# Batch 0 in two halves by queries: sparse attention and an ELU layer pair on one Trainium2 core

## The chip, the core and the metric

The kernel runs on one core of one Trainium2 chip. The metric is device microseconds (us) from the launch's first to its last work, and less is better. A run of the profiler gives one execution's trace; times of other executions are taken without it. Names of engines as in the profile: PE is the matmul engine (PEld its weight loads), DVE the vector engine, ACT the scalar engine, POOL and SP the two that issue most of the transfers. "DMA" is the set of 16 transfer engines.

## What is computed

Eight batches of 576 tokens with 8 heads of 64 go through attention with two fixed masks; the result, 4608 tokens of 512, goes through two dense layers with an ELU between them.

```python
mask_local = (rel >= 0) & (rel < 32)                       # heads 0..3
mask_strided = (rel >= 0) & (pos[None, :] % 32 == pos[:, None] % 32)   # heads 4..7
attn = softmax(where(mask, q @ k.T / 8, -1e9));  x = attn @ v
h = x @ w_in                                               # 4608x512 @ 512x2048
out = where(h > 0, h, exp(min(h, 0)) - 1) @ w_out          # 2048x512
```

Inputs and output are float32; the kernel computes in bf16 and loads with a cast on the way.

## The kernel before

**Tiling.** A token is numbered p*8+s with s in 0..7 (`NS`) and p in 0..71 (`RS`). Strided heads attend only within groups of equal token number modulo 32, local heads within a band of 32. A batch has four head pairs: `s0`, `s1` (strided) and `l0`, `l1` (local); each pair's queries are taken in two parts u = 0, 1. For batches 0 and 1 (`NPE`), q and k are transposed on PE (L409) and copied out of PSUM by ACT or DVE (L427); for batches 2 to 7 SP issues transposing transfers (`dma_T`, L670). Scores go to PSUM (`scores` L444, `scores_packed` L469), ACT takes the exponential (L498, L518), DVE multiplies by the mask (L504, L524), PE multiplies by v and by ones (`pv` L590), ACT takes log and exp(-log) of the sums (L622, L628), and DVE writes the scaled product into `xT` (`write_x` L634), the left operand of layer 1.

Layer 1 (`l1`, L682) works in nine chunks of 512 tokens. A chunk has 16 row blocks m of `w_in`; each takes 4 matmuls of 512 columns into one of the eight PSUM banks. ACT takes exp (L692), ACT or DVE clamps (L697), DVE takes the maximum with h (L707) and writes `g`, of which there are two tiles. Layer 2 (`l2`, L717) takes 16 matmuls of 512 columns for 128 tokens, needs all four quarters of `w_out`, and ends in a copy by ACT or DVE (L725) into one of four output buffers (`p_osb`) and a store (L731), which SP issues as two or three transfers, since the rows of a token group lie apart in the output.

**Order.** Nothing is scheduled by a planner at run time. `ORDER` (L37 to L145) is a list of about 2,600 tokens; each engine runs its instructions in the order in which the tokens stand there, and semaphores do the rest. The letters:

- D load (POOL issues it), X transposing transfer (SP), K/k cast of q/k by DVE/ACT, T transposes on PE, c/C copies of them by DVE/ACT
- S or P scores, e exp, m mask, O product with v, n log, r exp(-log), x write of x, V and W copies of v, F fills of masks and ones
- L (a and b its halves) layer 1, h exp, i/j clamp on DVE/ACT, g the maximum; Z layer 2 by quarters of the sum, o/q its copy by ACT/DVE, t its store; Y and y the last 128 tokens by halves of the output's columns
- w.7.28: 28 matmuls of zeros into bank 7

So `L.1.8.1` is chunk 1, m = 8, bank 1, and `Z.0.2.3.7` is tokens 256 to 383 of chunk 0, last quarter, bank 7. The token order couples things that do not depend on each other: a load that waits holds POOL's next loads, and a store that waits for its copy holds SP's next transposing transfers.

**Loads.** q and k of batch 0's first two strided heads come in float32 through SP and ACT in four transfers (L304), and are cast on the chip. All else is issued by POOL, in the order batch 0, most of batch 1, `w_in` (L266), `w_out`, batch 2 and so on. POOL has eight completion semaphores in rotation, so a load waits until the one eight before it has landed. SP's stores and transposing transfers have eight of their own.

In `before` batch 0 is loaded by pairs of heads, with all 72 rows p (80 where memory allows). Layer 1 of chunk 0 needs the first 512 tokens of batch 0 in the order s-major, so all four head pairs with both u.

Of the kernel before, what the change touches and what calls it, by code (L numbers as in the profile page):

```python
# [8 lines left out]
F32 = mybir.dt.float32  # L9
BF16 = mybir.dt.bfloat16  # L10
# [5 lines left out]
S = 576  # L16
D = 64
HG = 4
# [11 lines left out]

NPE = 2
# [11 lines left out]
T.1s1.q.7 r.0s1.0 x.0s1.0 e.0s0.1 c.1s1.q D.vl1.0 m.0s0.1 T.0l0.q.2 c.0l0.q O.0s0.0.34 D.vl0.0
r.0s1.1 x.0s1.1 n.0s0.0 O.0s0.1.67 n.0s0.1 r.0s0.0 S.0l0.1.01 x.0s0.0 F.k1 S.0l1.0.23 e.0l0.1
T.1s0.k.0 r.0s0.1 V.0.0 S.0l0.0.45 V.0.1 m.0l0.1 e.0l1.0 m.0l1.0 C.1s0.k O.0l1.1.23 e.0l0.0 D.kl.1
x.0s0.1 T.1l0.k.0 n.0l1.1 r.0l1.1 m.0l0.0 O.0l1.0.67 O.0l0.0.45 D.ql.1 D.wi0.0 c.1l0.k n.0l1.0
O.0l0.1.01 D.wj0.0 x.0l1.1 r.0l1.0 n.0l0.0 r.0l0.0 D.wi2.0 n.0l0.1 T.1l1.q.2 x.0l1.0 c.1l1.q r.0l0.1
D.vs.1 x.0l0.0 T.1l0.q.3 S.1s0.0.67 a.0.0.2 c.1l0.q x.0l0.1 e.1s0.0 T.1s1.k.5 a.0.1.3 b.0.0 m.1s0.0
T.1l1.k.4 C.1s1.k S.1s1.0.01 c.1l1.k S.1s0.1.67 b.0.1 h.0.0 a.0.3.4 b.0.3 e.1s0.1 a.0.2.7 i.0.0
h.0.1 g.0.0 D.wi1.0 S.1l0.0.56 e.1s1.0 h.0.3 S.1s1.1.01 m.1s0.1 i.0.1 m.1s1.0 e.1s1.1 e.1l0.0  # L50
D.wi3.0 b.0.2 h.0.2 g.0.1 a.0.9.2 b.0.9 D.vl.1 a.0.11.3 i.0.3 b.0.11 m.1s1.1 g.0.3 D.wo0.0 h.0.9
j.0.9 O.1s0.1.01 O.1s0.0.45 n.1s0.0 i.0.2 g.0.2 a.0.8.6 b.0.8 D.wo1.0 a.0.10.7 b.0.10 h.0.11 m.1l0.0
r.1s0.0 n.1s0.1 D.wo2.0 g.0.9 a.0.5.2 i.0.11 b.0.5 x.1s0.0 g.0.11 h.0.8 a.0.6.3 b.0.6 D.wo3.0
S.1l1.0.45 r.1s0.1 x.1s0.1 a.0.7.0 b.0.7 a.0.13.1 b.0.13 h.0.10 i.0.8 i.0.10 h.0.5 j.0.5 g.0.8 h.0.6
g.0.5 j.0.6 e.1l1.0 h.0.13 a.0.4.2 g.0.10 D.qs.2 g.0.6 m.1l1.0 V.1 i.0.13 b.0.4 S.1l0.1.34 h.0.7
S.1l1.1.56 e.1l0.1 e.1l1.1 i.0.7 a.0.12.7 b.0.12 D.ql.2 a.0.14.3 b.0.14 a.0.15.6 g.0.13 h.0.12
O.1s1.1.45 g.0.7 h.0.4 m.1l1.1 i.0.4 g.0.4 h.0.14 Z.0.0.0.0 b.0.15 n.1s1.1 r.1s1.1 x.1s1.1 j.0.12
g.0.12 h.0.15 O.1l0.0.12 D.ks.2 i.0.15 O.1s1.0.45 m.1l0.1 i.0.14 n.1l0.0 r.1l0.0 x.1l0.0 g.0.14
n.1s1.0 r.1s1.0 Z.0.0.1.0 X.qs.2 x.1s1.0 Z.0.2.0.7 Z.0.2.1.7 Z.0.2.2.7 g.0.15 D.kl.2 O.1l1.1.56
n.1l1.1 X.ks.2 O.1l1.0.34 n.1l1.0 r.1l1.1 x.1l1.1 X.ql.2 O.1l0.1.12 Z.0.0.2.0 Z.0.0.3.0 Z.0.2.3.7  # L60
n.1l0.1 X.kl.2 r.1l0.1 x.1l0.1 r.1l1.0 D.vs.2 x.1l1.0 L.1.8.1 L.1.5.2 h.1.5 L.1.14.3 i.1.5 h.1.8
L.1.15.4 o.0.2 h.1.14 g.1.5 L.1.7.5 q.0.0 L.1.4.2 j.1.14 i.1.8 g.1.14 L.1.10.0 h.1.4 L.1.2.3 h.1.2
h.1.7 L.1.3.7 i.1.4 D.qs.3 g.1.8 L.1.6.1 L.1.0.6 g.1.4 L.1.13.2 i.1.7 i.1.2 g.1.7 F.mx h.1.3 h.1.10
D.ks.3 g.1.2 j.1.10 D.vl.2 Z.0.3.0.5 Z.0.3.1.5 h.1.15 j.1.15 g.1.15 h.1.0 j.1.3 g.1.3 Z.0.1.0.4
X.qs.3 g.1.10 L.1.11.3 L.1.1.0 i.1.0 h.1.6 i.1.6 h.1.13 Z.0.1.1.4 Z.0.1.2.4 g.1.0 j.1.13 g.1.6
D.kl.3 h.1.11 g.1.13 h.1.1 i.1.1 g.1.1 t.0.2 j.1.11 P.2.4.67 e.2p.4 m.2p.4 P.2.1.12 e.2p.1 Z.0.1.3.4
o.0.1 Z.0.3.2.5 P.2.2.67 e.2p.2 P.2.3.01 g.1.11 W.2 P.2.0.34 m.2p.1 m.2p.2 e.2p.0 Z.0.3.3.5 m.2p.0
e.2p.3 m.2p.3 L.1.12.6 h.1.12 L.1.9.7 O.2s0.0.23 O.2s0.1.01 q.0.3 h.1.9 i.1.9 j.1.12 g.1.9 Z.1.0.0.4
Z.1.0.1.4 Z.1.3.0.5 n.2s0.0 g.1.12 t.0.0 r.2s0.0 x.2s0.0 n.2s0.1 O.2s1.0.67 r.2s0.1 n.2s1.0 r.2s1.0
V.2 Z.1.3.1.5 O.2l0.1.23 x.2s0.1 x.2s1.0 n.2l0.1 r.2l0.1 Z.1.0.2.4 Z.1.0.3.4 O.2s1.1.67 Z.1.3.2.5  # L70
t.0.3 n.2s1.1 r.2s1.1 O.2l1.1.01 q.1.0 x.2l0.1 Z.1.1.0.4 n.2l1.1 r.2l1.1 O.2l1.0.23 n.2l1.0 r.2l1.0
Z.1.1.1.4 x.2s1.1 O.2l0.0.67 Z.1.1.2.4 Z.1.1.3.4 D.ql.3 n.2l0.0 r.2l0.0 x.2l1.1 X.ks.3 P.3.4.01
e.3p.4 Z.1.3.3.5 x.2l1.0 x.2l0.0 L.2.11.0 h.2.11 q.1.1 m.3p.4 i.2.11 g.2.11 L.2.15.4 t.0.1 L.2.6.2
h.2.15 i.2.15 g.2.15 X.kl.3 X.ql.3 h.2.6 L.2.2.3 P.3.1.01 h.2.2 q.1.3 P.3.3.67 i.2.2 L.2.10.4
L.2.5.5 e.3p.1 D.vs.3 D.vl.3 j.2.6 L.2.4.0 h.2.10 m.3p.1 L.2.7.1 D.qs.4 g.2.2 D.kl.4 W.3 e.3p.3
h.2.4 j.2.4 g.2.6 O.3s0.1.67 n.3s0.1 r.3s0.1 i.2.10 g.2.10 L.2.1.2 h.2.1 g.2.4 L.2.13.3 L.2.9.0
h.2.7 m.3p.3 j.2.7 t.1.1 x.3s0.1 Z.1.2.0.4 P.3.2.67 D.ks.4 Z.1.2.1.4 i.2.1 g.2.1 g.2.7 L.2.8.1
D.ql.4 h.2.5 j.2.5 h.2.13 L.2.3.2 t.1.3 e.3p.2 g.2.5 h.2.8 i.2.13 g.2.13 h.2.3 P.3.0.56 e.3p.0
X.qs.4 L.2.0.3 h.2.0 i.2.8 g.2.8 j.2.0 h.2.9 X.ks.4 X.ql.4 m.3p.2 Z.1.2.2.4 Z.1.2.3.4 O.3l1.0.56
X.kl.4 n.3l1.0 i.2.3 g.2.3 O.3l0.1.12 D.vs.4 n.3l0.1 L.2.14.7 g.2.0 i.2.9 g.2.9 r.3l0.1 q.1.2  # L80
Z.2.0.0.3 r.3l1.0 Z.2.1.0.0 D.vl.4 m.3p.0 h.2.14 j.2.14 x.3l0.1 L.2.12.4 h.2.12 O.3s1.1.12 Z.2.0.1.3
x.3l1.0 n.3s1.1 g.2.14 r.3s1.1 O.3l1.1.67 i.2.12 Z.2.1.1.0 g.2.12 D.ks.5 n.3l1.1 r.3l1.1 O.3s1.0.45
n.3s1.0 t.1.0 Z.2.0.2.3 x.3s1.1 x.3l1.1 r.3s1.0 Z.2.0.3.3 O.3s0.0.12 n.3s0.0 x.3s1.0 P.4.4.67
Z.2.1.2.0 O.3l0.0.45 q.2.0 D.ql.5 Z.2.1.3.0 r.3s0.0 e.4p.4 P.4.2.67 n.3l0.0 x.3s0.0 r.3l0.0 m.4p.4
# [733 lines left out]
```

## Time and profile before

| | us |
|---|---|
| median of 3 runs (307.39 to 309.43) | 308.45 |
| the profiled execution, its own time | 308.96 |
| its span, first to last instruction | 307.3 |
| PE busy | 296.8 |
| ACT busy | 231.8 |
| DVE busy | 222.5 |
| POOL busy | 81.2 |
| first layer 1 matmul starts at | 23.26 |
| last matmul ends at | 303.2 |

The profile has a page (busy time, the span in 40 slices of 7.7 us, the chain of work that ended last, groups of instructions by line), and views that are asked of the trace: the timeline (merged instructions in order of time), busy time by stretches, waits. PE's busy time counts the modelled length of each matmul, 380 ns for 512 columns, while consecutive ones start much closer together; what PE has to spare is read from the distances between starts, not from the busy share.

### The profile page before, as it was taken

How to read it: one execution, taken by the hardware profiler on the slowest of the kernel's cores; microseconds unless marked ns; L12 is line 12 of the kernel's file. 1: busy time of each engine (PE TensorE's matmuls, PEld its weight loads, DVE VectorE, ACT ScalarE, POOL GpSimd, SP SyncE). 2: the span in 40 equal slices, each digit the busy share in tenths (PEclk: the TensorE clock that was granted, in tenths of full speed). 3: DMA queues.
4: the chain of work that ended last, by engine and by line, in shares of the span. 5: the costliest groups of instructions: out<-in, count | busy, mean ns of one | idle time of the engine just before them, and what ended most of it. 6: DMA issues, size and time to landing. Idle time of an engine off the chain costs nothing.

```text
span 307.3 us, 6136 instructions
## 1 busy us (share of the span) xinstructions
PE 296.8 (97%) x2316; PEld 151.8 (49%) x2316; DVE 222.5 (72%) x418; ACT 231.8 (75%) x396; POOL 81.2 (26%) x111
## 2 busy tenths in 40 slices
PE   5999999999999979999999999999999999999994
PEld 5774444445544545445444554544545544444452
DVE  4688993888689986998796777788678458973220
ACT  3798975779979997988897999966897459655321
POOL 8764323484083046092030092000000000000000
PEclk9999999999999999999999999999999999999999
DMA  8999999999999999999999199560020012101124
GB/s 156 198 195 206 195 202 160 213 198 167 234 119 139 125 162 152 228 126 128 185 151 155 36 131 152 65 156 14 20 73 0 20 51 68 36 0 34 36 68 137
DMA packets 107655, 37.58 MB, mean 122 GB/s; under 512 B 89099, under 2 KB 103147, under 8 KB 107627
## 3 DMA queue, kind: packets, MB, share of 16 engines
q0 software_dynamic: 70192, 19.43, 65.3%
q1 hardware_dynamic: 36998, 17.37, 30.0%
q10 hardware_dynamic: 436, 0.40, 0.5%
q8 instruction: 18, 0.29, 0.4%
q14 instruction: 11, 0.08, 0.1%
HBM read 39.47 MB, written 9.44 MB: 159 GB/s over the span
## 4 chain that ended last, share of the span: by engine, by line
PE 77%; DMA 9%; DVE 5%; ACT 2%; issue 2%; SPq 2%; POOL 2%; ACTq 0%; POOLq 0%; DVEq 0%
PE ps L687 34%; PE ps L721 33%; DMA kTl<-kl 4%; DMA ql<-in_q_dram 4%; PE ps L493 2%; PE ps L577 2%; SPq L680 2%; DVE xT L657 2%; DMA g<-in_q_dram 1%; PE ps L584 1%; PE ps L747 1%; PE ps L466 1%; POOL kl L243 1%; ACT ln L626 1%; PE ps L423 1%
## 5 line engine op out<-in xcount | busy, mean ns | idle before, releaser
L687 PE MATMUL ps<-xT,w_in_sb 128*128 128x512 bf16 x576 | 134.2, 380 | 0.4 <-DVE g L715 0.2
L721 PE MATMUL ps<-w_out_sb,g 128*128 128x512 bf16 x560 | 131.9, 379 | 0.0
L695 ACT ACTIVATE he<-ps 128x512 f32<-128x512 f32 x144 | 81.9, 595 | 24.2 <-PE ps L687 23.1
L687 PEld LDWEIGHTS <-w_in_sb 128*128 128x128 bf16 x576 | 54.2, 98 | 62.4 <-issue 1.1
L721 PEld LDWEIGHTS <-g 128*128 128x128 bf16 x560 | 52.4, 98 | 58.0
L715 DVE TENSOR_TENSOR g<-he,ps 128x512 bf16<-128x512 bf16 x95 | 64.0, 682 | 2.1
L657 DVE TENSOR_TENSOR xT<-ps,ln 64x576 bf16<-64x576 f32 (+1 forms) x64 | 43.3, 678 | 21.0 <-ACT ln L632 20.0
L704 DVE TENSOR_SCALAR he<-he 128x512 bf16<-128x512 f32 x95 | 40.4, 434 | 18.2 <-ACT he L695 17.7
L626 ACT ACTIVATE ln<-ps 64x576 f32<-64x576 f32 (+1 forms) x64 | 37.1, 584 | 11.7 <-PE ps L577 5.1
L632 ACT ACTIVATE ln<-ln 64x576 f32<-64x576 f32 (+1 forms) x64 | 39.7, 622 | 1.7
L713 DVE SCALAR_TENSOR_TENSOR g<-he,ps 128x512 bf16<-128x512 bf16 x49 | 32.9, 682 | 8.3 <-ACT he L702 8.0
L702 ACT ACTIVATE he<-he 128x512 bf16<-128x512 f32 x49 | 30.5, 629 | 2.6 <-DVE g L715 1.2
L502 ACT ACTIVATE e<-ps 128x1008 bf16<-128x1008 f32 (+1 forms) x30 | 27.0, 934 | 5.2 <-PE ps L493 5.1
L236 POOL DMA_DIRECT2D ql<-in_q_dram x24 | 20.1, 845 | 17.7 <-DMA qTl<-ql 11.9
L243 POOL DMA_DIRECT2D kl<-in_k_dram x24 | 17.9, 752 | 17.8 <-DMA kTl<-kl 13.4
L727 ACT COPY osb<-ps 128x512 f32<-128x512 f32 x17 | 9.9, 585 | 14.8 <-PE ps L721 14.7
L515 DVE TENSOR_TENSOR pm<-e,mask_x 128x1008 bf16<-128x1008 bf16 x24 | 16.2, 677 | 6.8 <-ACT e L502 6.8
L727 DVE COPY osb<-ps 128x512 f32<-128x512 f32 x18 | 12.3, 686 | 8.9 <-PE ps L721 8.8
L522 ACT ACTIVATE e<-ps 72x576 bf16<-72x576 f32 (+1 forms) x16 | 10.0, 646 | 2.4 <-PE ps L466 2.1
L577 PEld LDWEIGHTS <-vsp 72*128 72x128 bf16 x192 | 9.1, 98 | 5.2 <-issue 0.4
L584 PEld LDWEIGHTS <-vl 128*128 128x128 bf16 x144 | 8.6, 97 | 5.6 <-issue 0.6
L230 POOL DMA_DIRECT2D vs<-in_v_dram x8 | 5.4, 680 | 22.3 <-DVE vsp L667 21.0
(94 smaller groups left out, 177.6 us busy)
## 6 DMA issues: line engine op xcount, KB each, us to landing
out_dram<-osb SPq DMA_DIRECT2D x31, 144.0 KB
w_out_sb<-in_moe_w_out_dram POOLq DMA_DIRECT2D x4, 512.0 KB, 17.8
vl<-in_v_dram POOLq DMA_DIRECT2D x7, 288.0 KB, 11.2
ql<-in_q_dram POOLq DMA_DIRECT2D x24, 72.0 KB, 6.6
kl<-in_k_dram POOLq DMA_DIRECT2D x24, 72.0 KB, 5.4
qs<-in_q_dram POOLq DMA_DIRECT2D x5, 320.0 KB, 8.5
ks<-in_k_dram POOLq DMA_DIRECT2D x5, 320.0 KB, 7.2
vs<-in_v_dram POOLq DMA_DIRECT2D x5, 320.0 KB, 8.3
```

The lines of the kernel that those rows point to most:

```text
L502: nc.scalar.activation(e[0:R, :, 0:n], tiles.pop(("S", key, j))[0:R], ACT.Exp, scale=scale)
L626: nc.scalar.activation(t, s_ps, ACT.Ln)
L632: nc.scalar.activation(t, t, ACT.Exp, scale=-1.0)
L657: nc.vector.tensor_mul(dst, o_ps, rc)
L687: nc.tensor.matmul(tiles["h", ch, m], lhsT=w_in_sb[:, c, m * 128:(m + 1) * 128], rhs=xT[:, c, ch * CHUNK:(ch + 1) * CHUNK], start=(c == 2) ...
L695: nc.scalar.activation(e, tiles["h", i[0], i[1]], ACT.Exp)
L702: nc.scalar.activation(e1, e, ACT.Relu, bias=1.0, scale=-1.0)
L704: eng.tensor_scalar(e1, e, scalar1=1.0, scalar2=1.0, op0=ALU.min, op1=ALU.subtract)
L713: nc.vector.scalar_tensor_tensor(dst, e1, -1.0, h, op0=ALU.mult, op1=ALU.max)
L715: nc.vector.tensor_tensor(dst, e1, h, op=ALU.max)
L721: nc.tensor.matmul(ops, lhsT=g[ch % 2][:, m, kk * 128:(kk + 1) * 128], rhs=w_out_sb[:, m, :], start=(m == 0), stop=(m == MC - 1), skip_gro ...
L727: eng(o_sb, tiles.pop(("o", int(ch), int(kk))))
```

## The change

Batch 0 is cut by queries into p < 32 (`RA`, 256 tokens) and 32 <= p < 72 (`RB`, 320 tokens). Since a query sees only earlier tokens, the first half needs only the first 32 rows of q, k and v. Each half is loaded, transposed, scored and written to `xT` by itself, in the column order half, s, p. The first half packs the four heads on the partitions (4 x 32 rows), for which there are new masks. Layer 1 runs in chunks of 256, 320, 448 and then seven of 512; layer 2 stays at 128 tokens. `g` becomes one ring of 1024 columns.

The raw halves of batch 0 lie in `w_out_sb`, so the loads of `w_out` follow their transposes; batch 1's raw strided v lies in the raw buffer of local k, which batch 2 uses next. The first 256 columns of `w_in` are loaded first of all on POOL; then come half 0, `w_in` and half 1 in turns, `w_out`, and batch 1 among and behind it. The 28 matmuls of zeros go. The list of tokens is new from end to end.

```diff
+RA = PRE
+RB = RS - RA
+NA = NS * RA
+NB = NS * RB
+CH = ((0, NA), (NA, NB), (S, 2 * CHUNK - S)) + tuple(
+    (i * CHUNK, CHUNK) for i in range(2, 9))
...
-K.q.1 D.qs1.0 F.ms w.7.28 k.q.0 k.k.0 T.0s0.q.0.0 T.0s0.q.1.1 T.0s1.q.5 c.0s0.q.0 k.k.1 T.0s0.k.2.1
...
+D.wi0.0 k.k T.0s.k.6.0 K.q F.ms T.0s.q.2.0 C.0s.k.0 c.0s.q.0 S.0s.0.67 e.0s.0 F.sa D.kl0.0
+T.0l.k.2.0 D.ql0.0 D.vl0.0 D.vs0.0 m.0s.0 D.vl1.0 D.ks1.0 F.m1 F.ml T.0l.q.0.0 c.0l.q.0 D.wj0.0 F.la
+F.lb C.0l.k.0 S.0l1.0.01 e.0l1.0 V.0.0 F.k1 m.0l1.0 S.0l0.0.67 e.0l0.0 O.0s.0.34 m.0l0.0 n.0s.0
+r.0s.0 x.0s.0 O.0l.0.67 T.0s.k.5.1 c.0s.k.1 n.0l.0 D.qs1.0 D.wi1.0 r.0l.0 T.0s.q.0.1 C.0s.q.1 x.0l.0
+L.0.1.2 V.0.1 L.0.2.3 L.0.3.4 h.0.1 S.0s0.1.01 i.0.1 g.0.1 S.0s1.1.56 h.0.2 i.0.2 g.0.2 h.0.3 i.0.3
...
-Z.8.0.3.6 Z.8.2.2.1 Z.8.2.3.1 Y.8.3.0.7 q.8.2 o.8.0 y.8.3.0 t.8.2 Z.8.1.1.4 Z.8.1.2.4 t.8.0
-Z.8.1.3.4 o.8.1 t.8.1 Y.8.3.1.5 y.8.3.1
...
+t.7.1 i.9.6 g.9.6 Z.8.1.1.0 Z.8.2.1.1 Z.8.0.1.3 Y.8.3.0.2 o.7.2 Z.8.0.2.3 Z.8.0.3.3 Z.8.2.2.1
+Z.8.2.3.1 o.8.0 t.7.2 y.8.3.0 t.8.0 o.8.2 Z.8.1.2.0 Z.8.1.3.0 o.8.1 Y.8.3.1.4 q.7.3 t.7.3 t.8.2
+y.8.3.1 t.8.1
...
-    g = [consts.tile([128, MC, CHUNK], BF16, tag=f"g{i}", name=f"g{i}") for i in range(2)]
+    g = consts.tile([128, MC, 2 * CHUNK], BF16, tag="g", name="g")
...
-    raw1["vs"] = g[1][0:RP, 0:HG * NS * D // CHUNK, :].rearrange("p a b -> p (a b)")
-    stage = g[0][0:RP, 0:8, :].rearrange("p a b -> p (a b)").bitcast(F32)
+    raw1["vs"] = raw["kl"][0:RP]
+
+    part = ({nm: w_out_sb[:, i, :] for i, nm in enumerate(("qs", "ks", "ql", "kl", "vs"))},
+            {nm: w_out_sb[0:2 * RB, 8 + 2 * i:10 + 2 * i, :]
+             for i, nm in enumerate(("qs", "ks", "ql", "kl"))})
+    stage = {nm: g[:, i, :].bitcast(F32) for i, nm in enumerate("qk")}
...
+    def load_first(nm, u):
+        x = {"q": q, "k": k, "v": v}[nm[0]]
+        if nm == "vl":
+            n = HG * LB // 2
+            nc.gpsimd.dma_start(
+                out=blocks(vl_t[0], HG * LB)[PRE:128, u * n:(u + 1) * n],
+                in_=v[0, 2 * u:2 * u + 2].rearrange("h (t p) d -> p (h t) d", p=LQ))
+        elif nm == "vs":
+            if u == 0:
+                nc.gpsimd.dma_start(out=part[0][nm], in_=rows_first(x, nm))
+            else:
+                load_runs(nm, 0)
+        elif u == 0:
+            for i in range(2):
+                nc.gpsimd.dma_start(out=part[0][nm][2 * RA * i:2 * RA * (i + 1)],
+                                    in_=pair_first(x, nm, i, 0, RA))
+        else:
+            for i in range(2):
+                nc.gpsimd.dma_start(out=part[1][nm][:, i], in_=pair_first(x, nm, i, RA, RB))
...
-    for u in range(2):
-        load_stage(nc.sync, 0, u, q)
-        load_stage(nc.scalar, 1, u, k)
+    nc.sync.dma_start(out=stage["q"], in_=rows_first(q, "qs"))
+    nc.scalar.dma_start(out=stage["k"], in_=rows_first(k, "ks"))
...
+    def scores_first(key, u, bk):
+        i, j = int(bk[0]), int(bk[1])
+        p0, R = half(u)
+        c = key[1]
+        n = NA // 2 if key == "0s" else NS * R
+        sc = tiles["S", key, u] = ps[:, i:j + 1:j - i, 0:n]
+        qt, kt = qT[0][c], kT[0][c]
+        if key == "0s":
+            for sp in range(NS // 2):
+                for h in range(HG):
+                    for z in range(2):
+                        pr = slice(z * D, (z + 1) * D)
+                        q0 = (h * NS // 2 + sp) * RS
+                        k0 = h // 2 * KSY + (h % 2 * NS // 2 + sp) * RS
+                        nc.tensor.matmul(
+                            sc[h * RA:(h + 1) * RA, z, sp * RA:(sp + 1) * RA],
+                            lhsT=kt[pr, k0:k0 + RA], rhs=qt[pr, q0:q0 + RA],
+                            start=True, stop=True, skip_group_check=True)
+            return
...
     def l1(ch, m, cs, bk=None):
         ch, m = int(ch), int(m)
+        c0, n = CH[ch]
         if bk is not None:
-            tiles["h", ch, m] = ps[:, int(bk), :]
+            tiles["h", ch, m] = ps[:, int(bk), 0:n]
         for c in cs:
             nc.tensor.matmul(
                 tiles["h", ch, m], lhsT=w_in_sb[:, c, m * 128:(m + 1) * 128],
-                rhs=xT[:, c, ch * CHUNK:(ch + 1) * CHUNK],
+                rhs=xT[:, c, c0:c0 + n],
                 start=(c == 2), stop=(c == 1), skip_group_check=True)
```

The functions for transposes, copies, exponentials, masks, products and writes of batch 0 have such a second form each (`transposes_first`, `copy_first`, `exp_first`, `mask_first`, `pv_first`, `write_first`), which works on one half. In counts of PE instructions: batch 0 has 88 transposes for 96, 92 score matmuls for 56 and 108 products for 72; layer 1 has 640 matmuls (64 each of 256, 320 and 448 columns, 448 of 512) for 576; the 28 of zeros are gone; layer 2 and batches 1 to 7 keep theirs.

Elsewhere in the new list: the transposing transfers of a batch stand behind other stores than before. Before, `X.kl.3` follows the store `t.0.1`, whose copy comes after nearly all of layer 1 of chunk 1; after, it follows `t.0.0`, and `t.1.3` is the last store before batch 4's four transposing transfers. At the end, the copy `q.7.3` stands behind `Y.8.3.1` and takes the output buffer that the store `t.8.0` reads; on SP, `t.7.3`, `t.8.2`, the last half's store and `t.8.1` follow it, nine transfers in all.

More of the change, by code (lines that the diff above doesn't have):

```diff
@@ L43 @@
[L43 to L48, printed above, removed]
@@ L278, in load @@
         elif b == 0:
-            y = int(what[2])
-            if nm == "vl":
-                load_vpair(0, y)
-            else:
-                load_runs(nm, 0, 2 * y, 2)
+            load_first(nm, int(what[2]))
         elif nm == "vl":
@@ new lines, in pv_local_first @@
+    def pv_local_first(y, u, o, s):
+        p0, R = half(u)
+        pm = tiles.pop(("pm", f"0l{y}", u))
+        vb = blocks(vl_t[0], HG * LB)
+        for x in range(2):
+            nc.tensor.matmul(s[x * D:(x + 1) * D], lhsT=ones, rhs=pm[:, x],
+                             start=True, stop=True, skip_group_check=True)
+        for w, p, m in items_first(u):
+            for x in range(2):
+                ov, pv_ = (z.rearrange("k (s p) -> k s p", s=NS)[:, :, p - p0:p - p0 + m]
+                           for z in (o[x * D:(x + 1) * D], pm[:, x]))
+                nc.tensor.matmul(ov, lhsT=vb[:, (2 * y + x) * LB + w, :], rhs=pv_,
+                                 start=True, stop=True, skip_group_check=True)
@@ L409, in transposes, with write_first @@
+    def write_first(key, u):
+        _, s_ps, o_ps = tiles.pop(("O", key, u))
+        rc = tiles.pop(("rc", key, u))
+        c = 2 if key[1] == "s" else 0
+        n = slice(0, 2) if u == "0" else slice(int(key[2]), int(key[2]) + 1)
+        n = slice(c + n.start, c + n.stop)
+        nc.vector.tensor_mul(xT[:, n, 0:NA] if u == "0" else xT[:, n, NA:S], o_ps, rc)
     def transposes(key, nm, bank, u=None):
+        if key[0] == "0":
+            return transposes_first(key[1], nm, bank, u)
         P = Pair(key)
@@ L715, in elu, with g_of, l2 @@
             nc.vector.tensor_tensor(dst, e1, h, op=ALU.max)
[L717 to L718 removed]
+    def g_of(ch, kk, m):
+        c0 = (int(ch) * CHUNK + int(kk) * 128) % (2 * CHUNK)
+        return g[:, m, c0:c0 + 128]
+    def l2(ch, kk, i, bk):
+        ch, kk, i = int(ch), int(kk), int(i)
         ops = tiles["o", ch, kk] = ps[:, int(bk), :]
[L720 removed]
+        for m in range(i * 4, i * 4 + 4):
             nc.tensor.matmul(
[L722 removed]
+                ops, lhsT=g_of(ch, kk, m),
                 rhs=w_out_sb[:, m, :], start=(m == 0), stop=(m == MC - 1), skip_group_check=True)
```

425 lines of the change are left out of this document (293 added, 132 removed).

## The prediction

> **What bounds the kernel now.** I read the page's slices first, then the costliest groups, the chain of waits, and the timeline at the three places that the chain names: the start, 79 to 115 us, and the end.
>
> ```profile
> PE   5999999999999979999999999999999999999994
> DMA  8999999999999999999999199560020012101124
> ...
> L687 PE MATMUL ps<-xT,w_in_sb 128*128 128x512 bf16 x576 | 134.2, 380 | 0.4 <-DVE g L715 0.2
> L721 PE MATMUL ps<-w_out_sb,g 128*128 128x512 bf16 x560 | 131.9, 379 | 0.0
> ```
>
> PE is at 9 tenths in all but the first, one middle and the last slice, and the transfers are at 9 tenths until about 170 us. The 380 ns of a matmul are its modelled length. What it costs is the distance between starts, which the chain gives:
>
> ```profile
> 50.06 10.36 PE ps L687 x48
> ...
> 79.26 4.84 DMA kTl<-kl
> ...
> 106.85 8.38 DMA kTl<-kl
> ...
> 301.47 1.76 PE ps L747 x16
> ```
>
> 48 matmuls in 10.36 us are 0.216 us each, and 16 of 256 columns in 1.76 us are 0.11. The two layers are 1136 x 0.216 + 32 x 0.109 = 248.9 us (0.109 from the timeline's starts), the same in both kernels as the total of columns stays. PE's last end is at 303.2, so 54.3 us are something else: 23.3 up to the first layer 1 matmul; 5.9 more that the timeline shows lost to batch 1's attention from there to 65 us; about 25.1 in batches 2 to 7. To lower the time, one of these or the 4.1 us behind PE's end must shrink.
>
> ```profile
> 1.06 3.17 PE L399 MATMUL ps<-zero 128*128 128x128 bf16 x28 [1.06 <-DVE zero L308]
> ...
> 7.57 1.16 PE L420 MATMUL ps<-identity,ks 72*128 72x72 bf16 x16
> ...
> 13.10 0.66 PE L420 MATMUL ps<-identity,xT 72*128 72x72 bf16 x8
> ...
> 17.93 0.40 PE L466 MATMUL ps<-qTl,kTl 64*128 64x96 bf16 x5 [0.61 <-DVE xT L657]
> ...
> 24.02 0.43 PE L420 MATMUL ps<-identity,xT 72*128 72x72 bf16 x8
> ```
>
> The columns are start, length, instruction and count. Eight transposes take 0.66 us at 13.10 and 0.43 at 24.02. By their starts they are 60 ns apart until 23.7 and 30 after, so PE runs at half rate until about 23.9, though the clock row of the page does not show it. It was so right after the zero matmuls as well (16 in 1.16 us at 7.57), so these bought nothing, and I price their going at nothing.
>
> **The change, part by part.** All terms are against the profiled execution: 308.96 us, of which its span is 307.3; it lies 0.5 above the median.
>
> *Start.* Layer 1 can open when half 0 is written to `xT`. Two float32 transfers of 256 KB replace four of 160 KB, which landed at 4.6, 4.9, 5.8 and 6.1; between 320 KB at 4.9 and 640 KB at 6.1 I put 512 KB at 5.5. Then by rows of this trace: casts 0.6 to 6.2; eight transposes at half rate 0.9 to 7.1; copies 0.5 to 7.6; 32 scores at 30 ns 1.0 to 8.7; exp 0.4; mask 0.3 to 9.4. The other loads follow the order of issue at what queued ones cost before (0.8 us for 160 KB of bf16, 1.9 for a `vl` of 288 KB, 2.5 for 512 KB): `kl` 7.9, `ql` 8.5, v 9.3 to 10.7. DVE's copy V.0.0 needs both `vl` loads, and the masks of the other heads stand behind it. So the strided product ends at 12.4, its log, exp and write at 14.35, and the last local write at 15.85. Layer 1 opens at 15.9 (14.5 to 17.5) instead of 23.3.
>
> What before did ahead of 23.3 does not vanish. Half 1 has 152 small matmuls; in batches 2 to 7, 672 such take 21.1 us of spacing, 0.031 each, so 4.7 us. Batch 1 costs the 5.9 plus 72 transposes at 30 ns that stood ahead of 23.3: 8.1. To this comes the half rate, now under layer 1. Before, full rate came 0.7 us after the first layer 1 matmul but 6.0 after PE's last pause. Counted from the opening this leaves 0.35 us lost (half of 0.7), or 3.0 (half of 6.0); I take 2.0, nearer the second, as the work in those 6 us was unbroken too. By the Trainium skill, "TensorE: Matmul & The Clock Gate", section "Part 1: The HAM clock gate (the "warmup" mystery)", full speed comes after about 3.4 us of sustained work; an estimate by it is 1.7 lost, and the 3.17 us of zeros were just too short for it, which the 60 ns behind them bear out. Stalls of the new order: 0.5 (0 to 2). The sum is 15.9 + 4.7 + 8.1 + 2.0 + 0.5 = 31.2 against 23.3 + 5.9 = 29.2: **+2.0** (-1.5 to +5). It does not fall although layer 1 opens 7.4 us earlier, because the attention that half rate and waiting used to share with the loads now takes PE's time between matmuls of layer 1.
>
> What covers the rest: from 24 to 44 us DVE and ACT were busy 18.5 and 18.55 of 20, PE 19.99. After it they have about 22 and 20.5 us of work between 16 and 46, and half 1 adds 1.5 to 3 to each. If they fall behind, PE waits for `g`; that is in the stalls. The loads total the same; by the same rates `w_out`'s last quarter lands at 38 and batch 1's last at 44.8. PE needs `w_out` at about 38 (opening 15.9, layer 1 of 576 tokens 15.6, half 1 4.7, half rate 2.0) and batch 1 at about 54, another 15.6 later. The first has no slack, the second nine us less its attention. POOL's moved loads and mask fills stand ahead of nothing else that is late.
>
> *Middle.*
>
> ```profile
> 115.28 0.30 PE L493 MATMUL ps<-qTl,kTl 64*128 64x96 bf16 x6 [1.79 <-DMA kTl<-kl]
> ```
>
> PE waits 1.79 us for batch 4's transposed keys. The chain leads back to SP: batch 3's last transposing transfers stood behind a store at 77.70, POOL's loads waited for them until 84.65 (11.24 us by the timeline), and batch 4's four ran from 92 to 115. In the new order X.kl.3 follows an earlier store, and the last store ahead of batch 4's is ready at about 82.5. Four of them took 3.67, 5.20, 4.66 and 3.79, sum 17.3: done at about 100, needed at about 111. So **-1.8** (-2.4, by gaps beside it, to 0). Next late would be batch 5's, which before arrived in time with the same spacing.
>
> *End.* Before, the last 128 tokens' second half of columns (Y.8.3.1) is the last PE work, and SP has issued nearly everything by then:
>
> ```profile
> 299.32 4.88 SPq L739 DMA_DIRECT2D out_dram<-osb  x12
> 301.31 1.91 PE L747 MATMUL ps<-w_out_sb,g 128*128 128x256 bf16 x16
> 303.26 0.27 ACT L763 COPY osb<-ps 128x128 f32<-128x128 f32 x1 [1.12 <-PE ps L747]
> 303.55 0.29 DVE L764 COPY osb<-ps 128x128 f32<-128x128 f32 x1 [5.69 <-ACT osb L763]
> 303.88 0.65 ACTq L739 DMA_DIRECT2D out_dram<-osb  x1
> ```
>
> The span ends 5.8 us after that matmul's start. In the new order the copy q.7.3 and its store stand behind it, and q.7.3 takes the output buffer that t.8.0 empties. So DVE waits for t.8.0's landing, and SP holds t.7.3 (2 transfers), t.8.2 (3), the last half (1) and t.8.1 (3) behind that copy. With Y.8.3.1's start as zero: t.8.0's last issue at -0.95, landed at +1.15 (stores took 1.5 to 2.2), q.7.3 done at +1.9, nine issues on one queue at some 0.34 us (12 took 4.88) to +4.96, landing and closing 3.4 more: +8.4. **+2.6**. The low end, +0.5, is t.8.0 landing before the copy is called for; the high one, +3.2, a slower landing under nine transfers at once.
>
> *Other edits.* 64 more matmuls of layer 1 with fewer columns cost the constant part, about 2 ns each: 0.1. The ring of `g` lets chunk 2 begin without chunk 0 done; cover for what it saves or costs is the same PE work, 0.
>
> Sum: 2.0 - 1.8 + 2.6 = +2.8, profiled 311.8; less 0.5 for the median, **311.2**.
>
> **Rivals.** With 1% of 308.45 as what a measurement can tell, slower begins at 311.5 and faster ends at 305.4.
>
> A, the other side: half 0 is quicker. If V.0.0 does not hold the masks (v landed earlier, as its loads are only 0.8 us each and the queue is short), the strided and the local heads go side by side and the opening falls by their 3.4 us of log, exp and write, to 12.5. That gives 307.8; from 13.1 on or earlier it is not slower than before. For it: before, v landed about a microsecond after q and k. Against: two casts, eight transposes, copies and exp each in line leave no room before 11, and ACT is one queue.
>
> B: full rate comes late. If PE pauses in half 1 (it paused at 17.3 for a write of `xT` in before), the 6 us count anew from about 19 and full rate comes at 25, a loss of 4.5 instead of 2.0; each stall of PE for `w_out` or `g` adds 1. That is 314.5. For it: `w_out` has no slack. Against: layer 1 gives PE work to fill with.
>
> C: the wait for transposes comes back elsewhere (any batch whose last store waits for its copy): -1.8 becomes 0 or more, 313.0 to 314. For it: stores and transposing transfers still share SP. Against: twelve us of slack for batch 4.
>
> D: the end is not blocked, since t.8.0 lands before DVE comes to q.7.3: +0.5 instead of +2.6, 309.1. Against it: t.8.0 stands two copies ahead only.
>
> That the change does not do what it says I leave out: the loads of half 0 are in fact half as large.
>
> **How the numbers follow.** Forecast 0.42, A 0.16, B 0.18, C 0.12, D 0.12. The likeliest gives 311.2, its own range from the terms' middles 309 to 313. The range for 8 in 10 takes A's lower part (opening 10.5, or A with D: 305.7) and B's 314.5 with half a microsecond more of stalls: 305.3 to 315.3. Faster by over 1%: a third of A, a third of D (where the middle also gives 2.4), a little of the forecast: 0.12. Slower: all of B, most of C, 0.45 of the forecast: 0.47. Within 1%: 0.41.
>
> **What would show it.** The first layer 1 matmul at about 15.9 and transposes 30 ns apart only from 19 or later; layer 1's first 64 matmuls of 256 columns with half-1 work between; no wait of PE for `kTl<-kl` at 113; DVE waiting before the copy of q.7.3, and SP's last issue five us behind Y.8.3.1's start. It is wrong if the opening lies before 13 or after 18, if PE waits for `g` or `w_out` between 30 and 55, or if the span ends within 6.5 us of that start.

## The result and the profile after

The changed kernel takes 324.1 us (median of 4, 322.76 to 326.07) against 308.28 before (median of 4): 1.052 times as long, 95% interval 1.045 to 1.058. The prediction was 311.2, with a range of 305.3 to 315.3. The profiled execution has a span of 320.7 us, 13.4 more than before; at 322.76 it is the lowest of its four, so a ledger of it explains 13.4 of the 15.8 us between the medians. All ratios and intervals leave out executions over 1.5% above the fastest of the same kernel.

The slices of the page, to be read against those of before:

```profile
PE   0448999999999999999999999999999999999990
DMA  5999999999999999989999992050111220003114
GB/s 87 110 132 189 207 206 194 145 219 173 175 117 187 154 121 195 164 160 196 138 126 220 157 172 59 15 130 3 33 35 33 67 65 0 0 3 98 33 51 115
...
L922 PE MATMUL ps<-xT,w_in_sb 128*128 128x512 bf16 (+3 forms) x630 | 134.9, 360 | 1.5 <-DVE xT L889 0.4
L962 PE MATMUL ps<-w_out_sb,g 128*128 128x512 bf16 x535 | 130.1, 379 | 2.2 <-issue 0.8
```

PE does nothing in the first slice of 8 us and little in the next two. The DMA row says 9 tenths in the second and third, but a busy engine is not a moving one: the GB/s row begins 87, 110, 132, 189, and that of the kernel before begins much higher:

```profile
GB/s 156 198 195 206 195 202 160 213 198 167 234 119 139 125 162 152 228 126 128 185 151 155 36 131 152 65 156 14 20 73 0 20 51 68 36 0 34 36 68 137
```

(35 of the 1,200 matmuls of the two layers are missing from this trace. The ledger below therefore takes the work from the program and only the times from the trace.)

The chain of waits of the changed kernel, its longest pieces:

```profile
2.49 10.45 DMA w_out_sb<-in_k_dram
...
15.37 7.78 DMA w_out_sb<-in_q_dram
...
24.23 11.01 DMA w_in_sb<-in_moe_w_in_dram
...
114.40 11.11 DMA kTl<-kl
...
311.29 1.76 PE ps L990 x16
```

Three loads in a row make the first 35 us (`w_out_sb` holds the raw halves of batch 0 then). A transfer of 64 KB takes 10.45 us to land, one of 80 KB 7.78.

With PE's work on the two layers taken out (248.7 us before, 248.8 after), the span falls into three parts: other time of PE up to the first scores of batch 2, from there to PE's end, and what follows.

| | before | after | difference | forecast |
|---|---|---|---|---|
| layer 1 opens at | 23.3 | 23.7 | +0.4 | -7.4 |
| start: other PE time up to batch 2 | 29.3 | 37.9 | +8.6 | +2.0 |
| middle: the same in batches 2 to 7 | 25.3 | 26.3 | +1.0 | -1.8 |
| end: behind PE's last matmul | 4.1 | 7.7 | +3.6 | +2.6 |

The start in the timeline of the changed kernel (start, length, engine, line, instruction, and in brackets the idle time ahead of it with what ended it):

```profile
7.93 0.62 ACT L445 CAST w_out_sb<-g 128x512 bf16<-128x512 f32 x1 [4.66 <-DMA g<-in_k_dram]
8.61 0.61 PE L467 MATMUL ps<-identity,w_out_sb 128*128 128x128 bf16 x4 [8.61 <-ACT w_out_sb L445]
10.83 0.43 DVE L445 CAST w_out_sb<-g 128x512 bf16<-128x512 f32 x1 [5.77 <-DMA g<-in_q_dram]
...
23.20 0.71 PE L467 MATMUL ps<-identity,w_out_sb 80*128 80x80 bf16 x8 [3.51 <-DMA w_out_sb<-in_q_dram]
23.71 2.66 PE L922 MATMUL ps<-xT,w_in_sb 128*128 128x256 bf16 x12
```

The two float32 transfers land at 7.9 and 10.8 us; the prediction had them at 5.5. And layer 1, whose input is written by 20.8, stands on PE behind half 1's transposes, which wait 3.51 us for their load.

### The profile page after: what moved, and what is told of

The parts are those of the page before. It is cut to its first block, busy times and chain, and to the rows that moved or that the text cites. A ratio compares the mean times of both kernels' runs of the same rounds, so it can differ in the third digit from the quotient of the medians.

```text
span 320.7 us, 6379 instructions
## 1 busy us (share of the span) xinstructions
PE 290.2 (90%) x2381; PEld 152.4 (48%) x2416; DVE 224.8 (70%) x445; ACT 235.2 (73%) x416; POOL 85.6 (27%) x117
## 4 chain that ended last, share of the span: by engine, by line
PE 60%; DMA 19%; ACT 8%; DVE 4%; issue 3%; POOL 3%; ACTq 0%; SPq 0%; DVEq 0%; POOLq 0%
PE ps L962 29%; PE ps L922 24%; DMA qTl<-ql 4%; DMA kTl<-kl 3%; DMA w_in_sb<-in_moe_w_in_dram 3%; ACT he L930 3%; DMA w_out_sb<-in_k_dram 3%; DMA kl<-in_k_dram 3%; DMA w_out_sb<-in_q_dram 2%; PE ps L717 2%; DVE g L952 2%; ACT ln L856 2%; ACT ln L862 1%; PE ps L805 1%; PE ps L990 1%
## 5 line engine op out<-in xcount | busy, mean ns | idle before, releaser
L922 PE MATMUL ps<-xT,w_in_sb 128*128 128x512 bf16 (+3 forms) x630 | 134.9, 360 | 1.5 <-DVE xT L889 0.4
L930 ACT ACTIVATE he<-ps 128x512 f32<-128x512 f32 (+3 forms) x160 | 82.6, 551 | 21.9 <-PE ps L922 20.9
L922 PEld LDWEIGHTS <-w_in_sb 128*128 128x128 bf16 x640 | 61.4, 99 | 60.1 <-issue 2.1
L952 DVE TENSOR_TENSOR g<-he,ps 128x512 bf16<-128x512 bf16 (+3 forms) x104 | 64.4, 630 | 2.9
L939 DVE TENSOR_SCALAR he<-he 128x512 bf16<-128x512 f32 (+3 forms) x104 | 40.5, 401 | 21.5 <-ACT he L930 20.9
L856 ACT ACTIVATE ln<-ps 64x576 f32<-64x576 f32 (+3 forms) x62 | 36.9, 598 | 10.8 <-PE ps L805 4.6
L950 DVE SCALAR_TENSOR_TENSOR g<-he,ps 128x512 bf16<-128x512 bf16 (+3 forms) x56 | 34.8, 632 | 10.2 <-ACT he L937 10.0
L862 ACT ACTIVATE ln<-ln 64x576 f32<-64x576 f32 (+3 forms) x62 | 39.1, 634 | 1.6
L937 ACT ACTIVATE he<-he 128x512 bf16<-128x512 f32 (+3 forms) x56 | 32.7, 588 | 1.5 <-DVE he L939 0.3
L968 ACT COPY osb<-ps 128x512 f32<-128x512 f32 x20 | 11.6, 582 | 17.9 <-PE ps L962 16.8
L968 DVE COPY osb<-ps 128x512 f32<-128x512 f32 x15 | 10.3, 688 | 17.4 <-DMA out_dram<-osb 14.8
L467 PE MATMUL ps<-identity,w_out_sb 80*128 80x80 bf16 (+1 forms) x24 | 2.8, 278 | 14.5 <-ACT w_out_sb L445 8.6
L245 POOL DMA_DIRECT2D ks<-in_k_dram x6 | 4.1, 685 | 26.8 <-DMA kTs<-ks 23.8
```

Of the source, the lines that this page charges most:

```text
L856: nc.scalar.activation(t, s_ps, ACT.Ln)
L862: nc.scalar.activation(t, t, ACT.Exp, scale=-1.0)
L922: nc.tensor.matmul(tiles["h", ch, m], lhsT=w_in_sb[:, c, m * 128:(m + 1) * 128], rhs=xT[:, c, c0:c0 + n], start=(c == 2), stop=(c == 1), s ...
L930: nc.scalar.activation(e, tiles["h", i[0], i[1]], ACT.Exp)
L937: nc.scalar.activation(e1, e, ACT.Relu, bias=1.0, scale=-1.0)
L939: eng.tensor_scalar(e1, e, scalar1=1.0, scalar2=1.0, op0=ALU.min, op1=ALU.subtract)
```

## The experiments

What the prediction had wrong most is when loads land, so that came first. Counting packets in the trace by size gave a theory. The kernel before moves 367 packets of 4 bytes in its first 30 us, the changed one 6,973. Of these, 302 and 6,964 are POOL's; 302 fits 16 for each of the transfers that have run by then, of the 26 that POOL has issued. If a transfer whose outermost run is two heads uses 2 of the 16 engines, and each of the other 14 gets a 4-byte packet for every row that a working engine moves, then 4 transfers of 2x32 rows, 8 of 2x40 and one of 4x32 (half 0's v) make 4 x 14 x 32 + 8 x 14 x 40 + 12 x 32 = 6,656 extra. The difference of the two counts is 6,606, and the changed kernel issues other transfers in that time than the one before. The rival was that the number of small transfers and their order set the landings.

**Rows outermost in all first loads of q and k, in the float32 pair alone, and in POOL's alone.** The heads and rows p of the first loads of q and k change places, and the copies behind the transposes read PSUM in that order:

```diff
-    [[step * S * D, 2], [NS * D, n], [1, NS * D]]      # POOL's pairs of heads
+    [[NS * D, n], [step * S * D, 2], [1, NS * D]]
-    [[S * D, HG], [NS * D, RA], [1, NS * D]]           # SP's q, ACT's k
+    [[NS * D, RA], [S * D, HG], [1, NS * D]]
```

> Edit: in the first loads of q and k (both halves of batch 0) the row p becomes the outermost run of the transfer instead of the head; sizes, number and order of the transfers stay, and the copies behind the transposes put the columns back in order. Theory 1 (spread): a transfer with 2 or 4 heads outermost goes through 2 or 4 of the 16 DMA engines, the rest get one packet of 4 bytes for each row. With rows outermost the 4-byte packets fall by about 6,300, the two float32 transfers land at about 5.5 us instead of 7.9 and 10.8, layer 1 opens at 16 to 18 instead of 23.7, and the time is 315 to 319. Theory 2 (number and order): POOL's 0.7 us for each of the 17 transfers issued before wi1, its limit of eight in flight, and the 256 KB of w_in in front set the landings. Then layer 1 still opens at 22 or later and the time is above 322.

> Edit: only the two float32 transfers of SP and ACT get rows outermost; POOL's stay as they are. Theory 1: these two land at about 5.5 us, and what they no longer hold up on four engines (w_in's first part, the first k) lands about 3 us earlier too; the pairs of heads still go through 2 engines each. Layer 1 opens at about 20 to 21.5, time 320 to 322. Theory 2: the two land earlier, but POOL's loads do not, the opening stays at 22 or later, the time above 322.

> Edit: only POOL's twelve transfers of q and k by pairs of heads get rows outermost; the two float32 transfers stay. Theory 1: 4-byte packets fall by about 6,300; the float32 transfers still land at about 8 and 10.8; half 1's q is there at about 19 instead of 23.2 and no longer holds PE, so layer 1 opens at 20 to 21, the last part of w_in lands before 32 instead of 35, time 318 to 321. Theory 2: landings as in the changed kernel, opening at 23 or later, time above 322.

Measured: 317.32 us for both (ratio to before 1.030, 1.025 to 1.035), 321.08 for the float32 pair alone (1.041, 1.035 to 1.047), 321.44 for POOL's alone (1.043, 1.037 to 1.049). So 6.8, 3.0 and 2.7 us are gained on the changed kernel's 324.1, which was timed in another batch (the kernel before took 308.28 there and 308.73 here), and layer 1 opens at 16.7, 20.9 and 20.9. POOL's alone lies 0.4 above what was expected of it, the other two within. In the timeline of the first:

```profile
3.99 0.62 ACT L448 CAST w_out_sb<-g 128x512 bf16<-128x512 f32 x1 [1.22 <-DMA g<-in_k_dram]
...
5.10 0.72 DVE L448 CAST w_out_sb<-g 128x512 bf16<-128x512 f32 x1
...
12.18 0.61 PE L623 MATMUL ps<-pm,w_out_sb 32*64 32x32 bf16 x32 [0.94 <-DMA w_out_sb<-in_v_dram]
...
13.18 0.28 DVE L926 COPY vl<-vl 32x512 bf16<-32x512 bf16 x1 [2.45 <-DMA vl<-in_v_dram]
...
16.67 0.63 PE L953 MATMUL ps<-xT,w_in_sb 128*128 128x256 bf16 x2
```

The same bytes now land at 4.0, and DVE's cast at 5.10 does not wait for its transfer at all. POOL's 4-byte packets of the whole run fall from 13,296 to 7,408, by 5,888: not quite the 6,272 of the twelve transfers, because with 40 rows outermost 48 stay in each of eight (8 x 48 = 384). That fits 10 working engines with four rows of two heads each, and eight packets on each of the other six. The float32 pair, which does not go through POOL, leaves 8 packets of 4 bytes in the first 30 us of SP's and ACT's queues in the changed kernel, and 32 with rows outermost: 4 and 16 for each of the two transfers. The first theory holds; number, size and order of the transfers are unchanged in all three versions, so they don't explain the late landings.

**The same transfer alone, cut in different ways.**

> Nothing of the reference is computed: one transfer after another, each waited for by a copy of DVE, then one store. Each moves rows of 2 KB from q or k, given as c runs of m rows: through POOL with a cast to bf16 64 rows as 2x32, 4x16, 8x8, 16x4, 32x2 and 64x1, then 2x40, 40x2, 80x1, 72x1 and 71x1; through SP in float32 128 rows as 4x32, 32x4 and 128x1; every case twice. Theory 1: a transfer goes through as many of the 16 engines as the largest divisor of c up to 16 (2, 4, 8, 16, 16, 16; 2, 10, 16, 12, 1; 4, 16, 16) and each packet takes some 0.1 us there: 2x32 takes about 3 us longer than 16x4 or 64x1, 4x16 about 1.2, 8x8 about 0.4; 2x40 about 3.5 longer than 80x1; 71x1 about 6.5 longer than 72x1; in SP's, 4x32 about 2.5 longer than 32x4. Theory 2: only the bytes count: all cases of the same size within 0.5 us, and 71x1 as 72x1.

From the issue to the copy that waited for it (second of each pair): 2x32 5.03 us, 4x16 3.62, 8x8 2.82, 16x4 2.28, 32x2 2.29, 64x1 2.25; 2x40 5.37, 40x2 2.89, 80x1 2.51. Two of them in the timeline:

```profile
8.84 0.68 POOL L37 DMA_DIRECT2D t<-in_q_dram  x1 [6.56 <-DVE seen L38]
13.87 0.16 DVE L38 CAST seen<-t 64x8 f32<-64x8 bf16 x1 [5.34 <-DMA t<-in_q_dram]
...
29.16 0.51 POOL L37 DMA_DIRECT2D t<-in_q_dram  x1 [2.77 <-DVE seen L38]
31.44 0.16 DVE L38 CAST seen<-t 64x8 f32<-64x8 bf16 x1 [2.62 <-DMA t<-in_q_dram]
```

The first is 2x32, the second 16x4: 128 KB read either way, 2.75 us apart. In SP's float32 transfers, from one copy to the next, the second 4x32 took 5.0, the second 32x4 3.0 and 128x1 2.7. The 4-byte packets of one transfer were 464 for 2x32, 208 for 4x16, 80 for 8x8 and 16 from 16x4 to 64x1: 16, and on each idle engine one for every row that a working engine moves (14 x 32, 12 x 16, 8 x 8). The data packets show the same spread: of the 64 of a transfer at most 4 are under way at once in 2x32, 7 in 4x16, 12 in 8x8, and 19 to 23 from 16x4 on. One expected case missed: 71x1 took 2.42 us like 72x1 (2.41), not 6.5 longer, so single rows are dealt out over the engines whether or not their number divides. The Trainium skill, "DMA: Bandwidth & Descriptors", section "Why a DMA increments its semaphore by 16 and not by 1", states both: a transfer uses the largest number of engines up to 16 that divides the slowest dimension of both access patterns, and some of POOL's direct copies are an exception that is dealt out evenly. The counts and landings here agree (2, 4, 8, 16 and, for 40, 10 engines; 71 as the exception).

**Earlier stores at the end.**

```diff
-t.7.1 i.9.6 g.9.6 Z.8.1.1.0
+t.7.1 q.7.3 t.7.3 i.9.6 g.9.6 Z.8.1.1.0
...
-o.8.1 Y.8.3.1.4 q.7.3 t.7.3 t.8.2 y.8.3.1 t.8.1
+o.8.1 t.8.2 Y.8.3.1.4 t.8.1 y.8.3.1
```

> Edit: only the order of the end: the copy q.7.3 and its store stand before layer 2 of the last three groups, and t.8.2 and t.8.1 before the last half. If the span's last 3.6 us (it ends 9.4 us behind the start of the last half matmul, 5.8 in the kernel before) come from DVE's wait for the output buffer and nine stores behind it, the end falls to about 5.8 behind that start and the time to about 320.5. If the landing of the last stores takes that long by itself, the end stays at 8.5 or more and the time above 323.

Measured 320.31 (1.039, 1.034 to 1.044), 3.8 us gained; behind PE's end 3.9 us remain instead of 7.7. In the timeline of the changed kernel DVE waits as the prediction said:

```profile
308.75 8.49 SPq L982 DMA_DIRECT2D out_dram<-osb  x14
...
311.12 1.91 PE L990 MATMUL ps<-w_out_sb,g 128*128 128x256 bf16 x16
...
312.39 0.69 DVE L968 COPY osb<-ps 128x512 f32<-128x512 f32 x1 [14.06 <-DMA out_dram<-osb]
```

and with the new order SP is done earlier and DVE has only its quarter left:

```profile
309.19 5.25 SPq L982 DMA_DIRECT2D out_dram<-osb  x12
...
311.56 1.91 PE L990 MATMUL ps<-w_out_sb,g 128*128 128x256 bf16 x16
```

**Both together.**

> Edit: the changed kernel with rows outermost in all first loads of q and k (as in the first experiment) and with the earlier stores at the end (as in the fourth). If the start (6.8 us gained) and the end (3.8) are separate causes, the gains add up: 324.1 - 6.8 - 3.8 = 313.5. If the quicker start moves the end's wait elsewhere, less is gained, 315 or more.

313.1 (1.017, 1.013 to 1.021): the two causes add up. Start 31.3, middle 27.0, end 3.8: over the kernel before, 2.0 and 1.7 us more and 0.3 less. All that follows, except on the kernel before, is on top of this version.

**Zeros for full rate, in this version and in the kernel before.**

```diff
-D.wi0.0 k.k T.0s.k.6.0 K.q F.ms T.0s.q.2.0 C.0s.k.0
+D.wi0.0 w.5.33 k.k T.0s.k.6.0 w.5.6 K.q F.ms T.0s.q.2.0 w.5.6 C.0s.k.0
...
-w.7.28 k.q.0 k.k.0 T.0s0.q.0.0 T.0s0.q.1.1 T.0s1.q.5
+w.7.40 k.q.0 k.k.0 T.0s0.q.0.0 w.7.6 T.0s0.q.1.1 w.7.4 T.0s1.q.5
```

> Edit: the same, with 81 matmuls of zeros of 128 columns in PE's gaps before the opening (33 first of all, then 6, 6, 20 and 16), into a bank that nothing else uses then. If the half rate behind the opening costs what the prediction put there (2.0; full rate came 5.9 us behind the opening in the first experiment), dense work from 1 us on brings full rate before the opening and 1.5 to 3 us are gained on the kernel without them: 310.5 to 312. If zeros do not bring full rate, or the time before the opening is ACT's, DVE's and the loads', the time is the same within 0.7 or up to 1 us longer, since the zeros delay real work.

> Edit: the kernel before with 50 matmuls of zeros instead of 28: 40 in front, 6 and 4 between the first transposes, so that PE is dense from 1.06 to about 7 us. The prediction said that 28 bought nothing, since PE was still at half rate at 7.57. If 6 us of dense work bring full rate, transposes at 7 to 9 us are 30 ns apart instead of 60, layer 1 opens up to 2 us earlier and the time falls by 0.5 to 2, to about 307. If the small matmuls of attention that follow drop it back to half, or the loads set the pace, nothing changes within 0.7 us.

Neither gained. The first took 313.95 (1.020, 1.015 to 1.025), 0.85 more than without zeros by the medians. The second took 309.43 to 314.25 in four executions; the two that count give a ratio of 1.012 (1.002 to 1.021) to the kernel before, outside of both things expected, a gain or no change within 0.7 us. Zeros do bring full rate. In the kernel before with more of them:

```profile
7.01 0.83 PE L420 MATMUL ps<-identity,ks 72*128 72x72 bf16 x16
```

16 transposes take 0.83 us here, 1.16 there. But the trace's clock record (the stretches in which PE was granted full or half rate) shows full rate only from 4.97 to 11.79 and then half until 25.45, and layer 1 opens at 23.1 instead of 23.3. Most of what this execution lost (its span is 5.2 us longer) came far behind the zeros:

```profile
88.54 0.42 PE L493 MATMUL ps<-qTs,kTs 64*128 64x72 bf16 x8 [3.70 <-DMA kTs<-ks]
```

PE waits 3.70 us for batch 3's transposed strided keys, and the clock record has half rate again from 86.89 to 93.71. Whether the zeros brought that wait, and whether the other three executions had it, one trace can't tell, so the ratio of this version says little of the zeros themselves. In the other version it is full from 7.01 to 13.83, half to 20.66, and layer 1 opens at 15.9 instead of 16.8, with the start at 31.2 instead of 31.3: what is gained ahead of the opening is lost behind it. All lengths in the clock records but the last are multiples of 3.41 us (6.83 and 13.65 here, 283.3 in the kernel before). The Trainium skill, "TensorE: Matmul & The Clock Gate", section "Part 1: The HAM clock gate (the "warmup" mystery)", which the prediction cites, says that activity is judged in free-running windows of that length. The clock records agree, and by it the loss at half rate shifts with the phase from execution to execution. (Layer 1 opened at 16.7, 20.9, 20.9, 23.5 and 23.7 in five versions, and full rate came 5.9, 5.5, 3.4, 3.0 and 2.4 us later.)

**The first part of w_in behind half 0.**

```diff
-D.wi0.0 k.k ... m.0s.0 D.vl1.0 D.ks1.0
+k.k ... m.0s.0 D.vl1.0 D.wi0.0 D.ks1.0
```

> Edit: the version with rows outermost and the earlier stores at the end (313.1), and the first 256 KB of w_in behind half 0's loads instead of ahead of them. If what is left between the opening there (16.8) and the prediction's 15.9 is the landing of half 0 (its v came at 13.2, put at 10.7), half 0 lands about 1.3 us earlier (256 KB at some 200 GB/s) and layer 1 opens at 15 to 15.8, time 311.5 to 312.5. If the opening is set by ACT's and DVE's chain, or layer 1 then waits for w_in, the time is the same within 0.7.

312.94 (1.016, 1.011 to 1.020): the same. DVE's copy of v starts at 12.98 instead of 13.18, and layer 1 opens at 17.4. So the 256 KB ahead of half 0 were not what held v up. They stand ahead of half 1's loads now, and there PE waits 0.94 us for q, where it waited 0.25 without the edit.

**The middle: one store in the kernel before.**

```diff
-t.0.3 n.2s1.1 ... x.2l1.1 X.ks.3 P.3.4.01 ... t.0.1 ... X.kl.3 X.ql.3 h.2.6
+X.ks.3 X.kl.3 t.0.3 n.2s1.1 ... x.2l1.1 X.ql.3 P.3.4.01 ... t.0.1 ... h.2.6
```

> Edit: the kernel before with batch 3's transposing transfers of strided and local k ahead of one store, and that of local q ahead of another; nothing else. This is the prediction's term for the middle by itself: if PE's 1.8 us wait for batch 4's local keys at 115 comes from that store, POOL's loads of batch 4 start some 5 us earlier, the wait goes and the time falls by 1.5 to 2, to about 306.8. If the four transfers of batch 4 are late for another reason (the stores of chunk 1 in front of them, or the transfers' own 17 us), the wait stays above 1 us and the time within 0.7 of 308.6.

308.33 over ten executions (1.001, 0.999 to 1.003): the same. Yet in its profile the wait is gone:

```profile
73.30 2.12 SPq L680 DMA_TRANSPOSE kTl<-kl  x1
```

The transfer starts at 73.30 instead of 79.26, no wait of PE for `kTl` is left, and the middle is 23.4 us instead of 25.3. In that one execution the start is 30.5 instead of 29.3, full rate coming at 25.8 instead of 23.9. Whether the times don't show the gain because the wait isn't there in most executions of the kernel before, or because something else takes it back, one trace each can't tell. The wait of 1.8 us was read correctly; that it is worth 1.8 us of the median is not borne out.

**The middle: clamps from ACT to DVE.** The ten clamps of chunks 3 and 4 that are j tokens become i tokens in the same places.

> Edit: the version with rows outermost and the earlier stores (313.1), with the ten clamps of chunks 3 and 4 that ACT does (0.54 us each) given to DVE (0.34 each). Between 120 and 150 us ACT is busy 29 of 30 there and PE waits in places of 0.3 to 0.6 us. If the 1.7 us by which batches 2 to 7 cost PE more than in the kernel before come from ACT being behind, some 0.5 to 1.5 us are gained: 311.6 to 312.6. If they come from the order of the tokens or from transposing transfers, the time is the same within 0.5 or longer, since DVE is busy 9.7 of 10 between 100 and 110.

318.9 (1.035, 1.031 to 1.038): 5.8 us longer. The middle is 32.7 instead of 27.0. The timeline there:

```profile
129.58 1.10 DVE L970 TENSOR_SCALAR he<-he 128x512 bf16<-128x512 f32 x3 [1.89 <-ACT he L961]
...
131.32 1.89 PE L953 MATMUL ps<-xT,w_in_sb 128*128 128x512 bf16 x8 [1.74 <-DVE g L983]
...
135.51 0.86 DVE L970 TENSOR_SCALAR he<-he 128x512 bf16<-128x512 f32 x2 [2.13 <-ACT he L961]
...
137.22 1.04 PE L953 MATMUL ps<-xT,w_in_sb 128*128 128x512 bf16 x4 [1.90 <-DVE xT L920]
```

The clock record has half rate from 139.01 to 142.42, behind these two waits of PE. That is not what costs the 5.8 us, since two executions with a granted clock of 1.000 took 318.9 as well. A clamp on DVE waits for ACT's exponential at the head of DVE's queue, with the maxima and the writes of `xT` behind it; PE waits for those, and ACT, busy 4.8 of the 10 us from 130 on, waits for PE. It says nothing for or against ACT being behind in the version without it: the edit brought a queue's wait of its own.

## Why the prediction was wrong, step by step

Forecast was a span 2.8 us longer, measured 13.4. Of the 10.6 between them the start makes 6.6, the middle 2.8 and the end 1.0.

**The start, +2.0 forecast, +8.6 measured: the step that failed is the landing of the loads.** The prediction put the float32 pair at 5.5 between two rows and took "what queued ones cost before" for the rest (`kl` 7.9, `ql` 8.5, v 9.3 to 10.7). The rows it took these from were transfers with 80 rows or more outermost, on all 16 engines (as 80x1 alone, with its 16 packets of 4 bytes); the new ones have two or four heads outermost and go through as many engines. `kl` landed at about 12.9, half 1's q at 23.2, the last of `w_in` at 35.2. The Trainium skill's rule on dividing engines, cited above, put to the access patterns of the changed kernel, gives 2 and 4 engines; the prediction did not draw on it. Put right, this is worth 6.8 us in the medians, as the version with rows outermost shows. The prediction's remark that half 0's loads "are in fact half as large" was true and beside the point, and so was rival A, which wanted v earlier still. No rival named this one; B, the nearest in size (314.5), put it down to the clock. The sign it had named, an opening after 18, came true.

**The chain behind the landings held.** With rows outermost, the opening is 16.7 (forecast 15.9), late where v is late (13.2 against 10.7; why stays open, though half 0's strided v still has four heads outermost there, and PE waits 0.94 us for it). The strided product, which the prediction ended at 12.4, ran at 12.2 to 12.8. From the opening to batch 2, PE's other time is 32.3 - 16.7 = 15.6 us; the terms 4.7 + 8.1 + 2.0 + 0.5 make 15.3. So the claim that an earlier opening gains nothing by itself was right: in the version with both mends the start costs 31.3 us, 2.0 more than before. That this is the very term is partly luck: the opening, at 16.8, is 0.9 later than forecast, and what follows it, 14.5, is 0.8 less. Between 30 and 55 us PE waits there neither for `g` nor for `w_out`, as forecast.

**The middle, -1.8 forecast, +1.0 measured.** PE's wait for `kTl<-kl` shrank from 1.79 to 0.45:

```profile
125.55 0.30 PE L717 MATMUL ps<-qTl,kTl 64*128 64x96 bf16 x6 [0.45 <-DMA kTl<-kl]
```

The prediction counted what went and asked only for the next late transfer. Instead, smaller waits came: between 64 and 175 us the timeline of PE has eight, of 0.15 to 0.45 us, four of them for DVE, where that of the kernel before has two. Both sum to 2.0 us. But idle time is counted from a matmul's modelled end, 0.38 us after its start, while the next one could start after 0.216, so each wait costs some 0.16 us more than is shown, and six more of them an estimated 1.0. This would be the +1.0; it is argued and not shown, since a matmul that is missing from the trace leaves a gap too. In the version with both mends:

```profile
89.84 7.11 PE L953 MATMUL ps<-xT,w_in_sb 128*128 128x512 bf16 x31 [0.38 <-DVE xT L920]
...
102.91 0.42 PE L836 MATMUL ps<-pm,vsp 72*128 72x72 bf16 x8 [0.49 <-DVE pm L770]
...
134.21 0.41 PE L843 MATMUL ps<-pm,vl 128*128 128x96 bf16 x6 [0.26 <-DVE xT L920]
```

Which part of the new order brings them stays open: the one attempt to take work off ACT made a wait of its own. Rival C had a middle of 0 or more, but by transposing transfers behind late stores, of which only the 0.45 is left. And the wait that did go was worth nothing in the times, as the experiment on the kernel before shows.

**The end, +2.6 forecast, +3.6 measured: right.** The buffer's wait, the copy (312.39 to 313.08, so done 1.8 us behind the matmul's start at 311.29, forecast 1.9) and the nine issues behind it are there. Mis-sized was the issue: 0.46 us each instead of 0.34 (the prediction's own row, 12 in 4.88 us, gives 0.41), so the last ended 5.95 us behind that start, not 4.96. Rival D fell.

**The zeros.** "These bought nothing" was right for the time and incomplete as a reading: 50 of them do bring full rate, for one stretch of 6.8 us, and no version with more of them gained. The 28 may bring it at times: in 11 of 31 other executions of the kernel before, the granted clock was 0.967 to 0.978. The profiled one counts as 1.000 although it ran at half rate until 23.9, so these 11 must have reached full rate and lost it again. Their median is 307.6 us, that of the other 20 is 308.3, and the two overlap widely.

The range missed because its upper end added only known terms at their worst. The largest quantity without any row of its own, the rate of a transfer of a new shape, had no bound at all.

## What to carry to other kernels

When a load's access pattern changes, look at its outermost count before its bytes: 2 heads of 32 rows took 5.0 us where the same 64 rows cut 16x4 took 2.3, and in the kernel the late landing held everything behind it. A queue that runs in order charges an edit for what stands behind it: a store behind a copy that waits for a buffer cost 3.8 us, and ten clamps moved to the less busy engine cost 5.8. A wait in one profile is worth its length only if removing it shows in the times; here a wait of 1.8 us went and the median stayed.

## What the runs showed of the hardware that was not expected

- A transfer through POOL that leaves engines idle still sends each of them one 4-byte packet for every row that a working engine moves: 464 such packets for 2x32, 16 for 16x4. Their count in a trace tells how many engines carried the data.
- The DMA row of the page stood at 9 tenths in slices in which 110 and 132 GB/s moved, and at 9 tenths where 207 did. The GB/s row tells what the busy row does not.
- Full rate came at 4.97 and 7.01 us with dense zeros and was lost again at 11.79 and 13.83, with PE working but pausing between small matmuls.
- A wait of PE in the midst of dense work can come with lost clock: half rate for 6.83 us around a wait of 3.70, and for 3.41 behind two of 1.74 and 1.90. Around the kernel before's wait of 1.79 the clock record shows none.
